# 128-row first projections, lead-in loads on SyncE, and row copies moved or dropped in a memory-augmented attention and gated feed-forward training step

## The chip, the cores and the metric

One core of a Trainium2 chip runs the whole program: forward pass and all gradients in one launch. The metric is the device time of one execution in microseconds (us); below 0.3% a difference can hardly be told from none.

The core has five engines with a program of their own: TensorE (matmuls; PE in the profile, its weight loads PEld), VectorE (DVE), ScalarE (ACT), GpSimd (POOL) and SyncE (SP), which here only starts transfers. Transfers run on 16 DMA engines that all queues share. SyncE, ScalarE and GpSimd each start transfers in the order of their own program: what waits in such a queue holds back what is written behind it.

## The reference

```python
def _fwd_reference(A_x, A_mem0, A_Wq, A_Wk, A_Wv, A_Wo, A_seg_len, B_x, B_w1, B_w3, B_w2):
    xn = _layernorm(A_x)                                   # 2048 x 640
    s = _A_ref(xn, A_mem0, A_Wq, A_Wk, A_Wv, A_Wo, 32)
    g = _silu(_B_ref(xn, B_w1, B_w3, B_w2))                # gated feed-forward, F = 1728
    return A_x + s * g

# _A_ref: 64 segments of 32 tokens, one after another
for s in range(n_seg):
    h = concatenate([mem, xs])                             # 8 memory rows + 32 tokens
    q, k, v = h @ Wq, h @ Wk, h @ Wv                       # 32 heads of 128
    p = softmax(where(mask, q @ k.T * scale, -1e9))
    o = (p @ v) @ Wo
    mem = o[:8]; outs.append(o[8:])
```

The program returns this output and, for a given gradient of it, the gradients of x, mem0, Wq, Wk, Wv, Wo, w1, w3 and w2. All data are bfloat16. The eight memory rows make the 64 segments a chain, forward and again backward.

## The kernel before

The work runs in stages, and within each the order is written out by hand: `in_order` ties every instruction to the one before it on its engine. So the order of the calls in the source is the order of each queue.

**Feed-forward and layer norm** (`phase12_ln_Bfwd`, to about 285 us). Four blocks of 512 tokens; for each of 14 slices of the hidden width, `hidden` multiplies with w1 and w3, and `up` follows one block behind. The normalized rows go to DRAM as XN. Stores of `sl` (to SLT) are on SyncE, of `ds` (to DUT) and of the hidden block (to HB) on GpSimd. In block 3 `x_rows` (L252, L254) copies XN within DRAM into HRO, which has 120 rows per tile: 96 tokens of three segments, then their 24 memory rows. The stage ends with the projections of the first 672 tokens by Wv: `first_rows` (L367 the matmuls, L372 the store) for six blocks of 112 rows and four groups of 1024 columns, in two halves of 512. Here all halves use the PSUM tag `pg`, which has two buffers.

**First part** (`first_part`, 285 to 406 us). The same projections by Wk and then Wq. A counter n runs over the 48 calls of `first_rows`, and other work hangs on its values: fetches of Wq and Wo on ScalarE's queue, `turn_w` (TensorE turns a head of Wv, SyncE stores it to WVT), `kload` and `kturn` of the first keys, the load of vt. The stores go through GpSimd.

**Recurrence forward** (its last Wv matmuls at 1616 us) and **output rows** (to 1795 us), not touched. The recurrence uses `packed_half` (L307): the 32 rows of h against four column groups at once, each in its own 32 columns of the array.

**Recurrence backward** (`phase4_Abwd`, 1795 to 2994 us). A unit is one tile of 120 rows (tl) and four heads (qd). A lead-in works through 19 units: `ld` loads q, v, the gradient and the probabilities, `turn` transposes (its copy gvT has two buffers and is stored to VTD by GpSimd, L1268), `dprob`, `dsoft`, `gmem` follow. The first six units are loaded ahead. In the lead-in, the loads of QVM, QVS or QVX and PR are on GpSimd, that of the gradient and the store GXP (L1315) on SyncE. Then 64 steps of `chain` follow, with later units in their gaps. After each of the first steps from t = 53 downward, one transfer of the list `later` is started on GpSimd (L1406); the first two copy the rows of GS within DRAM into GWO, which is laid out like HRO. Each step stores its gOT stage to GOS on SyncE (L1157) and its eight memory rows to GWO.

**Attention weight gradients** (`phase6_Awgrads`, 2994 to 4224 us). For each of eight groups of four heads, 22 units: loads on SyncE, `s1` to `s4` on TensorE, then `wg` (L1562), which needs the rows hr (loaded from HRO in the first group, L1627). `ld_w` loads the turned weights of a group: Wv from WVT, Wk and Wq by a transposing DMA (L271) from the inputs. GWO is read at the end of the stage.

**Other gradients** (to 4795 us), not touched.

Of the kernel before, what the change touches and what calls it, by code (L numbers as in the profile page):

```python
# [10 lines left out]
F32 = mybir.dt.float32  # L11
# [29 lines left out]
class K:  # L41
# [109 lines left out]
    def setup_dram(self):  # L151
        tc = self.tc
        S, D, T, H, F = self.S, self.D, self.T, self.H, self.F
        HD = self.HD
        dp = self.ctx.enter_context(tc.tile_pool(name="scratch", bufs=1, space=bass.MemoryType.DRAM))
        self.dp = dp
        mk = lambda name, shape, dt=BF16: dp.tile(list(shape), dt, name=name, uniquify=False)
        self.XN = mk("XN", (S, D))
        self.SLT = mk("SLT", (F, S))
        self.DUT = mk("DUT", (F, S))  # L160
        self.HB = mk("HB", (F, S))
        self.DZ = mk("DZ", (S, D))
        self.GB = mk("GB", (S, D))
        self.GS = mk("GS", (S, D))

        self.NR = S + 8 * T
        self.GXA = mk("GXA", (S, D))
        self.HRO = mk("HRO", (self.NR, D))

        self.OT0 = 7  # L170
        self.NO = 4 * ((T - 1 - self.OT0) // 4)
        self.OTX = mk("OTX", (self.NO, P, H, 24))
        self.FS = mk("FS", (T, 64, 320))
        self.SR = mk("SR", (S, D))
        self.GWO = mk("GWO", (self.NR, D))


        self.QVS = mk("QVS", (T // 4, 4, 32, 4, 2, 1024))
        self.KS = mk("KS", (T // 4, 4, 32, 4, 1024))
        self.GOS = mk("GOS", (T // 4, 4, 32, 4, 1024))  # L180
        self.QM = mk("QM", (T, 8, HD))
        self.QVM = mk("QVM", (T, 8, 4, 2, 1024))
        self.NB0 = 672
        self.QVX = mk("QVX", (self.NB0, 2, HD))
        self.KX = mk("KX", (self.NB0, HD))
        self.GB0 = 1344
        self.GL = 2 * P
        self.GX0 = mk("GX0", (S - self.GB0, HD))
        self.OR = mk("OR", (self.NTL * 120, HD))
        self.PR, self.DSR, self.VTD = [], [], []  # L190
        self.GXP = mk("GXP", (self.NTL, P, 8, 3, 2, 32), F32)
        for tl in range(self.NTL):
            n = self.geo(tl)[3]
            self.PR.append(mk(f"PR{tl}", (n, H, P)))
            self.DSR.append(mk(f"DSR{tl}", (n, H, P)))
            ns, nm = self.geo(tl)[0:2]
            self.VTD.append(mk(f"VTD{tl}", (P, ns, H, 40)))
        self.PM = mk("PM", (T, P, 80))
        self.GSP = mk("GSP", (8, 3, 160, 512))
        self.WVT = mk("WVT", (P, H, D))  # L200

    def x_src(self, tl, w, c0, c1):
        return self.tok_src(96 * tl, self.geo(tl)[2], w, c0, c1)
# [43 lines left out]
        r = 120 * (t // 3) + self.geo(t // 3)[2] + 8 * (t % 3)  # L247
        return A[r:r + 8, :]

    def x_rows(self, A, X, eng):  # L250
        n = self.NTL - 1
        eng.dma_start(A[0:120 * n, :].rearrange("(t r) d -> t r d", r=120)[:, 0:96],  # L252
                      X[0:96 * n, :].rearrange("(t r) d -> t r d", r=96))
        eng.dma_start(A[120 * n:120 * n + 32, :], X[96 * n:self.S, :])  # L254


    def g_src(self, tl, c0, c1):
        nx = self.geo(tl)[2]
# [96 lines left out]
    return pt  # L355


def first_rows(k, ps, stage, xs, off, W, dst, x0, cg, nb=112, tag="b0pb", w=1024, q=None):

    nc = k.nc  # L360
    for b in range(2):
        c0 = cg * 1024 + b * 512
        if w == 512 or b == 0:
            st = stage()
        pb = ps.tile([nb, 512], F32, name="b0pb", tag=tag)
        for dc in range(k.DC):
            nc.tensor.matmul(pb[:], xs[:, dc, x0 - off:x0 - off + nb], W[:, dc, c0:c0 + 512],  # L367
                             start=(dc == 0), stop=(dc == k.DC - 1))
        s0 = b * 512 if w == 1024 else 0
        k.copy(st[:, s0:s0 + 512], pb[:], eng='vs'[b])  # L370
        if w == 512 or b == 1:
            (q or nc.sync).dma_start(dst[x0:x0 + nb, cg * 1024 + (b * 512 if w == 512 else 0):cg * 1024 + b * 512 + 512], st[:])  # L372


def phase3_Afwd(k, W4, Wv, Wk_):
# [18 lines left out]
def first_part(k, Wv, Wk_, Wq, Wo, kTs, vt, hxs, rest):  # L394
    nc, tc = k.nc, k.tc
    DC, H, HD = k.DC, k.H, k.HD
    with tc.tile_pool(name="b0", bufs=1) as io, tc.tile_pool(name="b0s", bufs=4) as stp, \
# [50 lines left out]
            turn_w()  # L448
        n = 0
        for W, dst in ((Wk_, k.KX[:, :]), (Wq, k.QVX[:, 0])):  # L450
            for x0 in range(0, k.NB0, 112):
                for cg in range(4):
                    if n % 2 == 1 and fetch:
                        nc.scalar.dma_start(*fetch.pop(0))
                    first_rows(k, ps, lambda: stp.tile([112, 1024], BF16, name="b0st", tag="b0st"), xs, 0, W, dst, x0, cg, q=nc.gpsimd)
                    turn_w()
                    if zero:
                        nc.gpsimd.memset(zero.pop(0)[:], 0.0)
                    if n >= 26 and n % 2 == 0 and (n - 26) // 2 < 9:
                        i = (n - 26) // 2  # L460
                        if i > 0:
                            kturn(i - 1)
                        if i < 8:
                            kload(i)
                    if n == 20:
                        mem_ld()
                    if n == 30:
                        assert not turns
                        nc.gpsimd.memset(kTs[1][:], 0.0)
                    if n == 44:  # L470
                        for i in range(2):
                            nc.sync.dma_start(vt[64 * i + 8:64 * i + 40, :], k.QVX[0:32, 1, 2048 * i:2048 * i + 2048])
                    n += 1
# [432 lines left out]
def phase3b_out(k, Wo, W0, W4):  # L906
# [12 lines left out]
    with tc.tile_pool(name="oio", bufs=1) as io, tc.tile_pool(name="oac", bufs=1, space=bass.MemoryType.PSUM) as pa, \  # L919
# [96 lines left out]
        while g0:  # L1016
# [2 lines left out]
        in_order(k, start)  # L1019
    WT["v"] = W4.tile([P, H, D], BF16, name="WvT", tag="w3")  # L1020

    n = k.NTL - 1
    later = [(k.GWO[0:120 * n, :].rearrange("(t r) d -> t r d", r=120)[:, 0:96], k.GS[0:96 * n, :].rearrange("(t r) d -> t r d", r=96)),
             (k.GWO[120 * n:120 * n + 32, :], k.GS[96 * n:k.S, :])]

    for s in range(3):
        t0 = (2, 0, 1)[s]
# [14 lines left out]
def phase4_Abwd(k, out2, WoT, WvT, WkT, WqT, later):  # L1042
# [3 lines left out]
    with tc.tile_pool(name="gst", bufs=1) as st, tc.tile_pool(name="gchain", bufs=1) as ch, \  # L1046
# [185 lines left out]
        def ld(tl, qd, eng=None):  # L1232

            ns, nm, nx, n = k.geo(tl)
            c0, h0 = qd * 512, qd * 4
            i = cnt["l"]
            cnt["l"] += 1
            early = i < len(pro)
            g = i % 6 if early else (i - len(pro) + 1) % NG
            if g < NG:  # L1240
                gor = gors[g][:]
                qv = fl.tile([120, 2, 512], BF16, name="gqv", tag="gqv", bufs=4)[:]
                Pr = fl.tile([120, 4, P], BF16, name="gPr", tag="gPr", bufs=4)[:]
            else:
                x = xb[:, g - NG]
                qv = x[:, 0:1024].rearrange("p (i c) -> p i c", i=2)
                gor = x[:, 1024:1536]
                Pr = x[:, 1536:2048].rearrange("p (h c) -> p h c", h=4)
            t0 = 3 * tl
            q = nc.gpsimd if early else nc.sync  # L1250
            q.dma_start(
                qv[nx:n], k.QVM[t0:t0 + ns, :, qd // 2, :, 512 * (qd % 2):512 * (qd % 2) + 512].rearrange("t r i c -> (t r) i c"))
            k.load_x(qv, 0, k.x_src(tl, "qv", c0, c0 + 512), q)
            k.load_x(gor, 0, k.g_src(tl, c0, c0 + 512), nc.sync)
            q.dma_start(Pr[0:n], k.PR[tl][:, h0:h0 + 4, :])
            uu["l", tl, qd] = qv, gor, Pr

        def turn(tl, qd):
# [152 lines left out]
def phase6_Awgrads(k, X, out0, out3, out4, out5):  # L1411
# [12 lines left out]
    with tc.tile_pool(name="h6i", bufs=3) as io, tc.tile_pool(name="h6", bufs=1) as hp, \  # L1424
# [20 lines left out]
        def ld_w(qd):  # L1445
            c0 = qd * 512
            ws = []
            for i, src in enumerate((k.A_Wv, k.A_Wk, k.A_Wq)):
                w = gp.tile([P, 4, D], BF16, name="w6", tag=f"w6{i}")
                if i == 0:  # L1450
                    nc.sync.dma_start(w[:], k.WVT[:, 4 * qd:4 * qd + 4, :])
                else:
                    turned_load(k, w[:], src.rearrange("d h e -> d (h e)")[:, c0:c0 + 512])
                ws.append(w)
# [146 lines left out]
        for qd in range(8):  # L1601
            u0 = NTL * qd
            for p in range(NTL):
# [20 lines left out]
                    spill(qd, p - 5)  # L1624
                if 6 <= u < 11:
                    c = 4 * (u - 6)
                    nc.sync.dma_start(hr[0:120, c:c + 4], k.HRO[120 * c:120 * c + 480, :].rearrange("(t p) d -> p t d", p=120))  # L1627
                if u == 11:
                    nc.sync.dma_start(hr[120:P], k.HRO[120 * NF:k.NR, :].rearrange("(t r) d -> r t d", r=8))
                if p % 11 == 2:  # L1630
                    out_ld(2 * qd + p // 11)
                if p % 11 == 6:
# [84 lines left out]
def phase12_ln_Bfwd(k: K, Wv, Wk_):  # L1717
# [6 lines left out]
    with tc.tile_pool(name="bw", bufs=1) as wp, tc.tile_pool(name="bio", bufs=2) as io, \  # L1724
# [128 lines left out]
        for blk in range(NBLK):  # L1853
            for fc in range(FC):
# [20 lines left out]
                if fc == 9:  # L1875
                    fetch((blk + 1) % NBLK)
                if blk == 3 and fc == 2:
                    k.x_rows(k.HRO, k.XN, nc.sync)
                if blk > 0:
                    if fc == 0:  # L1880
                        hidden_out(blk - 1)
# [5 lines left out]
                            up_ld(blk - 1, fc // 2 + 1)  # L1887
        hidden_out(NBLK - 1)
        xb = io.tile([P, DC, BLK], BF16, name="xnT_b", tag="xnT_b")
        turned_load(k, xb[:, :, 0:224], k.XN[448:672, :])  # L1890
        up_ld(NBLK - 1, 0)
        up_ld(NBLK - 1, 1)
        xa, off = xnTs[NBLK], 0
        stg = []

        def stage():
            stg.append(ln.tile([112, 512], BF16, name="b0st", tag=f"xt{len(stg) % 8}"))
            return stg[-1]
        for n, (x0, cg) in enumerate([(x0, cg) for x0 in range(0, k.NB0, 112) for cg in range(4)]):
            if n % 3 == 1 and n // 3 < TB:  # L1900
                up(NBLK - 1, n // 3)
                if n < 6:
                    up_ld(NBLK - 1, n // 3 + 2)
            if x0 == 448:
                xa, off = xb, 448
            first_rows(k, ps, stage, xa, off, Wv, k.QVX[:, 1], x0, cg, tag="pg", w=512)
        in_order(k, start)


# [271 lines left out]
```

## Time and profile before

Median of three runs 4798.12 us (4796.45 to 4808.65); the profiled execution took 4796.79 us, its span is 4795.1 us.

| stretch, us | what | TensorE busy, us | granted clock | DMA share |
|---|---|---|---|---|
| 180 to 190 | feed-forward, block 3 | 3.28 of 10 | 0.75 | 0.44 |
| 250 to 300 | Wv projections, change of stage | 43.30 of 50 | 1.00 | 0.41 |
| 300 to 350 | first part, Wk | 48.27 of 50 | 1.00 | 1.02 |
| 350 to 400 | first part, Wq | 50.00 of 50 | 1.00 | 0.47 |
| 1800 to 1810 | backward lead-in, start | 4.51 of 10 | 0.50 | 0.53 |
| 1840 to 1850 | backward lead-in | 5.54 of 10 | 0.83 | 1.10 |
| 2078 to 2110 | backward steps, GWO copy | 23.86 of 32 | 0.79 | 0.72, then 0.55 |
| 3000 to 3020 | weight gradients, start | 7.57 of 20 | 0.50 | 1.13, then 0.99 |
| 3110 to 3150 | wg of the first group | 39.84 of 40 | 1.00 | 0.24 |

The granted clock is the share of TensorE's full speed that it was given; the DMA share is the mean busy share of the 16 DMA engines (it can come out a little over 1). A line of the timeline gives start, duration, engine, source line, operation, output and input tiles, the number of instructions, and in brackets the idle time before it with what ended it. A line of the waits reads: who waited, for whom, us in total, times, longest. A line of a table by stretches gives TensorE, weight loads, VectorE, ScalarE and GpSimd busy us with counts, the clock, the DMA share and GB/s.

### The profile page before, as it was taken

How to read it: one execution, taken by the hardware profiler on the slowest of the kernel's cores; microseconds unless marked ns; L12 is line 12 of the kernel's file. 1: busy time of each engine (PE TensorE's matmuls, PEld its weight loads, DVE VectorE, ACT ScalarE, POOL GpSimd, SP SyncE). 2: the span in 40 equal slices, each digit the busy share in tenths (PEclk: the TensorE clock that was granted, in tenths of full speed). 3: DMA queues.
4: the chain of work that ended last, by engine and by line, in shares of the span. 5: the costliest groups of instructions: out<-in, count | busy, mean ns of one | idle time of the engine just before them, and what ended most of it. 6: DMA issues, size and time to landing. Idle time of an engine off the chain costs nothing. (4 is left out here: it accounts for less than half of the span.)

```text
span 4795.1 us, 160346 instructions
## 1 busy us (share of the span) xinstructions
PE 4474.0 (93%) x64434; PEld 2864.5 (60%) x64704; DVE 2248.3 (47%) x7164; ACT 1591.1 (33%) x4371; POOL 2109.1 (44%) x3541
## 2 busy tenths in 40 slices
PE   8898999999999787989999998899999999999999
PEld 4455555555555464656666665666666666667665
DVE  8634666666666524545555553332234322311460
ACT  5432555555544522323333332322233222300000
POOL 6522555555555405445544443643355433411340
PEclk9999999999999796999999999899999999999999
DMA  8763566666555497777777773943455433669774
GB/s 271 234 231 101 174 178 180 179 181 181 178 166 169 128 218 206 209 210 207 219 210 208 212 211 111 207 131 108 108 151 154 133 109 106 190 193 223 158 179 98
DMA packets 997844, 841.31 MB, mean 175 GB/s; under 512 B 542558, under 2 KB 880402, under 8 KB 995096
## 3 DMA queue, kind: packets, MB, share of 16 engines
q1 hardware_dynamic: 784201, 552.53, 41.9%
q0 software_dynamic: 130592, 229.98, 16.4%
q10 hardware_dynamic: 82307, 48.52, 3.9%
q8 instruction: 511, 8.37, 0.8%
q14 instruction: 233, 1.91, 0.1%
HBM read 473.80 MB, written 311.48 MB: 164 GB/s over the span
## 5 line engine op out<-in xcount | busy, mean ns | idle before, releaser
L1562 PE MATMUL wg<-gr,hr 128*128 128x512 bf16 x2352 | 519.1, 379 | 2.5
L1543 PE MATMUL g<-w,ghacc 128*128 128x320 bf16 x3072 | 459.8, 300 | 0.8
L1562 PEld LDWEIGHTS <-hr 128*128 128x128 bf16 x2400 | 233.9, 98 | 278.8
L1543 PEld LDWEIGHTS <-ghacc 128*128 128x128 bf16 x3072 | 288.4, 98 | 104.2 <-ACT ghacc L92 2.2
L307 PEld LDWEIGHTS <-hx 128*32 128x32 bf16 x7680 | 176.7, 96 | 168.9 <-issue 5.7
L90 DVE CAST wgo<-wg 128x512 bf16<-128x512 f32 x72 | 49.8, 692 | 471.3 <-PE wg L1562 462.9
L90 DVE CAST stg<-bank 128x512 bf16<-128x512 f32 x256 | 177.0, 692 | 161.4 <-PE bank L307 154.9
L778 POOL DMA_DIRECT2D OR<-xv x163 | 90.4, 555 | 354.0 <-ACT xv L92 334.0
L92 ACT COPY ghacc<-t6g 128x768 bf16<-128x768 bf16 (+1 forms) x176 | 137.2, 780 | 304.1 <-PE t6g L1525 303.1
L1508 POOL DMA_DIRECT2D GSP<-grs x48 | 25.7, 547 | 477.6 <-ACT grs L1500 474.8
L326 PEld LDWEIGHTS <-gkv 128*8 128x8 bf16 x8192 | 179.0, 87 | 89.0 <-issue 7.1
L1268 POOL DMA_DIRECT2D VTD<-gvT x176 | 129.4, 741 | 219.7 <-ACT gvT L1267 199.9
L730 POOL TENSOR_TENSOR xP<-xP,xrz 120x480 bf16<-120x480 bf16 x163 | 161.4, 990 | 75.1 <-DVE xrz L729 46.2
L710 ACT ACTIVATE xP<-xsp,xnm 120x120 bf16<-120x120 f32 (+1 forms) x540 | 186.6, 373 | 20.5 <-DVE xnm L692 17.2
L1549 DVE TENSOR_TENSOR ghacc<-ghacc,g 128x320 f32<-128x320 f32 x192 | 93.5, 487 | 210.0 <-PE g L1543 210.0
L92 ACT CAST wgo<-wg 128x512 bf16<-128x512 f32 x48 | 28.1, 586 | 479.8 <-PE wg L1562 421.4
L1297 DVE SCALAR_TENSOR_TENSOR gdS<-gdp,Dx,gPr 120x120 bf16<-120x120 f32 (+1 forms) x680 | 182.8, 331 | 0.0
L326 PE MATMUL bank<-Wo,oTm 128*32 128x320 bf16 x4032 | 158.2, 312 | 18.8 <-DVE oTm L608 18.8
L326 PE MATMUL gbank<-WvT,gkv 128*8 128x320 bf16 x4096 | 171.0, 311 | 4.6 <-issue 3.6
L1315 POOL DMA_DIRECT2D GXP<-gks x157 | 91.1, 581 | 190.9 <-ACT gks L1313 184.3
L326 PE MATMUL gbank<-WkT,gkv 128*8 128x320 bf16 x4096 | 163.9, 301 | 3.9 <-issue 2.1
L307 PE MATMUL bank<-Wq,hx 128*32 128x512 bf16 x2560 | 163.0, 384 | 2.6 <-DVE stg L90 2.6
(354 smaller groups left out, 10920.6 us busy)
## 6 DMA issues: line engine op xcount, KB each, us to landing
QVS<-stg SPq DMA_DIRECT2D x128, 256.0 KB
vTt<-VTD SPq DMA_DIRECT2D x64, 320.0 KB
VTD<-gvT POOLq DMA_DIRECT2D x168, 120.0 KB, 3.8
DSR<-gdS POOLq DMA_DIRECT2D x168, 120.0 KB, 3.2
dS<-DSR SPq DMA_DIRECT2D x168, 120.0 KB
P<-PR SPq DMA_DIRECT2D x168, 120.0 KB
PR<-xP POOLq DMA_DIRECT2D x163, 120.0 KB, 3.3
OR<-xv POOLq DMA_DIRECT2D x163, 120.0 KB, 3.1
```

Of the source, the lines that this page charges most:

```text
L90: return nc.vector.tensor_copy(out, in_)
L92: return nc.scalar.copy(out, in_)
L307: k.nc.tensor.matmul(bank[32 * g:32 * g + 32, :], x[:, dc, :], W[:, dc, c0:c0 + 512], start=(dc == 0), stop=(dc == k.DC - 1), tile_positio ...
L326: k.nc.tensor.matmul(pm[p0:p0 + nq, 0:320], x[:, h, :], W[:, h, 320 * b:320 * b + 320], start=(first and i == 0), stop=(last and i == 15), ...
L710: nc.scalar.activation(Pb[0:n, j, 0:n], sp[0:n, j, :], ACT.Exp, bias=nmx[0:n, j:j + 1], scale=k.scale, accum_out=Z[0:n, j:j + 1])
L730: eng.tensor_tensor(Pb[0:n, :, 0:n], Pb[0:n, :, 0:n], bc_last(rz[0:n], n), ALU.mult)
L1268: nc.gpsimd.dma_start(k.VTD[tl][:, :, h0:h0 + 4, :], vTq[:])
L1297: nc.vector.scalar_tensor_tensor(dS[0:n, j, 0:n], dp[0:n, j, :], Dx[0:n, j:j + 1], Pr[0:n, j, 0:n], op0=ALU.subtract, op1=ALU.mult)
L1315: (nc.sync if (tl, qd) in pro else nc.gpsimd).dma_start(k.GXP[tl, :, qd, 0:ns], ks[:].rearrange("p s i h m -> p s i (h m)"))
L1543: nc.tensor.matmul(pg[:], ring[:, i, j, r0:r0 + P], Ws[qd][i][:, j, 320 * h:320 * h + 320], start=(i == 0 and j == 0), stop=(i == 2 and j ...
L1549: nc.vector.tensor_tensor(a, a, pg[:], ALU.add)
L1562: nc.tensor.matmul(pw[:], hr[:, tl, dc * P:(dc + 1) * P], grs[i][:, tl, :], start=(tl == 0), stop=(tl == NF - 1))
```

## The change

Five edits. The first 672 tokens are cut into five blocks of 128 rows and a rest of 32 rows, which `last_rows` does packed, four column groups at once; in the feed-forward stage the two halves get a PSUM tag each. The values of n move with the smaller number of calls (42), and the last stores (n from 36) go through SyncE. The lead-in loads of QVS or QVX and of PR go through SyncE. The copy of XN into HRO is dropped but for the last two tiles; hr takes its 96 token rows from XN. The copy of GS into GWO is cut into eight pieces, one behind unit 18 of each head group (the seventh group has two, the last none), and in its old place the first head group of the turned Wk and Wq is stored to a new DRAM tensor WQK, from which `ld_w(0)` loads it. What the edits are for: fewer rows of the array left unused, a shorter GpSimd queue, and no large DRAM copies or transposing loads at points where the order of the work leaves little slack.

```diff
-def first_rows(k, ps, stage, xs, off, W, dst, x0, cg, nb=112, tag="b0pb", w=1024, q=None):
+def first_rows(k, ps, stage, xs, off, W, dst, x0, cg, tag="b0pb", w=1024, q=None):
...
-        pb = ps.tile([nb, 512], F32, name="b0pb", tag=tag)
+        pb = ps.tile([P, 512], F32, name="b0pb", tag=tag if isinstance(tag, str) else tag[b])
...
+def last_rows(k, ps, stage, xs, off, W, dst, tag="b0pb", w=1024, q=None):
+    x0 = k.NB0 - 32
+    for b in range(2):
+        if w == 512 or b == 0:
+            st = stage()
+        pb = ps.tile([P, 512], F32, name="b0pb", tag=tag if isinstance(tag, str) else tag[b])
+        packed_half(k, pb, xs[:, :, x0 - off:x0 - off + 32], W, b)
+        s0 = b * 512 if w == 1024 else 0
+        k.copy(st[:, s0:s0 + 512], pb[:], eng='vs'[b])
+        if w == 512 or b == 1:
+            c0, c1 = (b * 512 if w == 512 else 0), b * 512 + 512
+            (q or k.nc.sync).dma_start(dst[x0:k.NB0].rearrange("r (g c) -> g r c", g=4)[:, :, c0:c1], st[:])
...
-            for x0 in range(0, k.NB0, 112):
-                for cg in range(4):
+            for x0 in list(range(0, k.NB0 - 32, P)) + [None]:
+                for cg in range(4 if x0 is not None else 1):
...
+                    if x0 is None:
+                        last_rows(k, ps, stage, xs, 0, W, dst, q=nc.gpsimd if n < 36 else nc.sync)
+                    else:
+                        first_rows(k, ps, stage, xs, 0, W, dst, x0, cg, q=nc.gpsimd if n < 36 else nc.sync)
...
-    later = [(k.GWO[0:120 * n, :].rearrange("(t r) d -> t r d", r=120)[:, 0:96], k.GS[0:96 * n, :].rearrange("(t r) d -> t r d", r=96)),
-             (k.GWO[120 * n:120 * n + 32, :], k.GS[96 * n:k.S, :])]
+    later = [(k.WQK[i], WT[w][:, 0:4, :]) for i, w in enumerate("kq")]
...
-            k.load_x(qv, 0, k.x_src(tl, "qv", c0, c0 + 512), q)
+            k.load_x(qv, 0, k.x_src(tl, "qv", c0, c0 + 512), nc.sync)
             k.load_x(gor, 0, k.g_src(tl, c0, c0 + 512), nc.sync)
-            q.dma_start(Pr[0:n], k.PR[tl][:, h0:h0 + 4, :])
+            nc.sync.dma_start(Pr[0:n], k.PR[tl][:, h0:h0 + 4, :])
...
-                if i == 0:
-                    nc.sync.dma_start(w[:], k.WVT[:, 4 * qd:4 * qd + 4, :])
+                if i == 0 or qd == 0:
+                    nc.sync.dma_start(w[:], k.WVT[:, 4 * qd:4 * qd + 4, :] if i == 0 else k.WQK[i - 1])
...
-                    nc.sync.dma_start(hr[0:120, c:c + 4], k.HRO[120 * c:120 * c + 480, :].rearrange("(t p) d -> p t d", p=120))
+                    nc.sync.dma_start(hr[0:96, c:c + 4], k.XN[96 * c:96 * c + 384, :].rearrange("(t p) d -> p t d", p=96))
+                    nc.sync.dma_start(hr[96:120, c:c + 4], k.HRO[120 * c:120 * c + 480, :].rearrange("(t p) d -> p t d", p=120)[96:120])
...
+                if p == 18:
+                    if qd < 7:
+                        nc.gpsimd.dma_start(k.GWO[360 * qd:360 * qd + 360, :].rearrange("(t r) d -> t r d", r=120)[:, 0:96],
+                                            k.GS[288 * qd:288 * qd + 288, :].rearrange("(t r) d -> t r d", r=96))
+                    if qd == 6:
+                        nc.gpsimd.dma_start(k.GWO[120 * NTL - 120:120 * NTL - 88, :], k.GS[96 * NTL - 96:S, :])
...
-                    k.x_rows(k.HRO, k.XN, nc.sync)
+                    k.x_rest(k.HRO, k.XN, nc.sync)
...
-            first_rows(k, ps, stage, xa, off, Wv, k.QVX[:, 1], x0, cg, tag="pg", w=512)
+            first_rows(k, ps, stage, xa, off, Wv, k.QVX[:, 1], x0, cg, tag=("pg", "pu"), w=512)
+        last_rows(k, ps, stage, xb, BLK, Wv, k.QVX[:, 1], tag=("pg", "pu"), w=512)
```

## The prediction

> **What bounds the kernel now.** The page first: the busy table and the chain that ended last.
>
> ```profile
> PE 4474.0 (93%) x64434; PEld 2864.5 (60%) x64704; DVE 2248.3 (47%) x7164; ACT 1591.1 (33%) x4371; POOL 2109.1 (44%) x3541
> ```
>
> TensorE has work on record 93% of the span, so time can go in two ways only: fewer matmul microseconds, or fewer holes between them. I went through TensorE's timeline stage by stage where the diff touches it, then asked the waits and the queues of SyncE and GpSimd what ended each hole.
>
> The first projections run TensorE flat out, at a granted clock of 1.00:
>
> ```profile
> 376.77 4.49 PE L367 MATMUL b0pb<-Wq,b0x 128*112 128x512 bf16 x20
> 381.10 0.34 PE L443 MATMUL kpt<-ident,kr 96*128 96x96 bf16 x4
> 381.27 4.49 PE L367 MATMUL b0pb<-Wq,b0x 128*112 128x512 bf16 x20
> ...
> 414.53 1.25 PE L307 MATMUL bank<-Wv,hx 128*32 128x512 bf16 x20
> ```
>
> From 376.77 to 381.10 twenty matmuls take 4.33 us, 0.216 each, whether 112 rows are used or 128. The last line, from the recurrence, is the packed form: twenty matmuls of 32 rows, four side by side, follow one another every 1.19 us (414.53, 415.71 the next).
>
> The same projections with Wv, at the end of the feed-forward stage, have holes:
>
> ```profile
> 242.71 1.24 PE L367 MATMUL b0pb<-Wv,xnT_b 128*112 128x512 bf16 x5 [0.72 <-ACT b0st L92]
> 244.28 3.40 PE L367 MATMUL b0pb<-Wv,xnT_b 128*112 128x512 bf16 x15 [0.33 <-DVE b0st L90]
> ```
>
> Both halves share one PSUM tag of two buffers, and ScalarE is late while it serves `up`.
>
> The two copies from DRAM to DRAM leave the widest holes:
>
> ```profile
> 188.69 2.29 PE L1784 MATMUL pg<-xnT_b,w1s 128*128 128x512 bf16 x5 [6.67 <-DVE sl L1793]
> ```
> ```profile
> 2078.00:2094.00 16.00, 12.38 (x266) 7.68 (x263) 6.70 (x36) 3.94 (x13) 6.72 (x13) 0.79 0.72 245
> 2094.00:2110.00 16.00, 11.48 (x197) 7.00 (x199) 2.64 (x8) 4.14 (x13) 4.97 (x9) 0.79 0.55 168
> 2110.00:2126.00 16.00, 15.30 (x371) 10.16 (x365) 9.31 (x50) 5.46 (x19) 8.14 (x16) 1.00 0.78 228
> ```
> ```profile
> POOL GXP L1315 <- DMA GWO<-GS: 5.7, 1, 5.7
> ```
>
> The first hole follows the HRO copy (issued at 162.8, 2520 KB read and written again): VectorE waits for buffers whose stores stand in the full rings. The second begins where GWO<-GS is issued (2078.62): TensorE falls from 15.3 busy us of 16 to 12.4 and 11.5, and the clock from 1.00 to 0.79.
>
> The lead-in of the backward recurrence, and the start of the weight gradients:
>
> ```profile
> 1810.32 0.55 POOL L1255 DMA_DIRECT2D krb<-PR  x1
> 1810.86 0.58 POOL L1268 DMA_DIRECT2D VTD<-gvT  x1
> ```
> ```profile
> ACT gvT L1266 <- DMA VTD<-gvT: 39.4, 11, 9.1
> ```
> ```profile
> 3001.92 5.56 SPq L271 DMA_TRANSPOSE w<-in_A_Wk_dram  x1
> 3007.53 5.91 SPq L271 DMA_TRANSPOSE w<-in_A_Wq_dram  x1
> 3013.48 0.60 SPq L1462 DMA_DIRECT2D dS<-DSR  x1
> ```
> ```profile
> 3016.57 0.58 PE L1483 MATMUL t<-ident,dS 120*128 120x120 bf16 x4 [11.48 <-DMA dS<-DSR]
> ```
>
> GpSimd issues eighteen loads before its first VTD store, for which ScalarE then waits. Later, two weight transposes hold SyncE for 11.5 us, and the load for which TensorE idles 11.48 us stands behind them.
>
> **What the skill says.** "TensorE: Matmul & The Clock Gate", Part 3: four column tiles run at once, its three-tile case measured 2.38 times; this trace gives 4.33/1.19 = 3.6 times for four. Same page, Part 1: after an idle window of some 3.4 us the clock falls to half; agreed, the five matmuls behind the 6.67 us hole took 2.29 us against 1.24. "DMA: Bandwidth & Descriptors", section Issuing engines are not separate DMA queues: another issuing engine saves only sequencer time; so I give the move to SyncE nothing in bandwidth. No SyncE landing is listed in this trace, so for a load I use that page's fit (Anatomy of one DMA): 2.0 us + bytes/436 GB/s.
>
> **The change, part by part.**
>
> *1. Rows.* Per weight, 6 blocks x 8 halves x 5 = 240 matmuls become 5 x 8 x 5 = 200 plus two packed halves of 20. Before: 48 x 1.08 = 51.8 us. After: 40 x 1.08 + 2 x 1.19 = 45.6. Saved 6.2 per weight; all on the path, since TensorE is the engine that ends these stretches: 18.7 for three weights. Evictions fall from 48 to 42 halves per weight at 0.69 (VectorE) or 0.59 us (ScalarE) and stay hidden: a pair of halves takes 2.16.
>
> *2. Two PSUM tags for Wv.* The waits for b0st between 216 and 256 (0.70, 0.34, then 0.72 and about 0.33 three times) add up to 4.2 us; four banks cover them. Saved 4.
>
> *3. Give-back in the first part.* From 300 to 345 the DMA share is 1.01 to 1.06, at 370 to 414 GB/s, with TensorE full since 315. The same bytes must now move in about 7 us less, and Wq is needed 7 us earlier. Its last piece is issued at 315.4, its first use was 351.8; slack remains. The last stores go through SyncE, where two kr loads now stand behind stores that wait for evictions; the turn two chunks later (4.3 us) needs them. Cost 0 to 6; I take 2.
>
> *4. No HRO copy of the rows.* Gone: 6.67 and 1.47 us of holes, and 3.7 - 2.2 = 1.5 from the half clock afterwards: 9.7. Blocks 1 and 2 keep 1 to 1.8 at the same place without such a copy. Saved 8 (6 to 10). The later hr loads read the same bytes in ten loads instead of five: five more issues of 0.43 us on SyncE, spread over five units.
>
> *5. GWO copy moved.* The distances of the GOS stores, one per step, are 17.8, 31.5 and 13.0 around the copy, 62.3 for three steps; neighbours take about 17.0. Excess 11.2. The two WQK stores in its place move 640 KB each, an eighth of the copy's 5040 KB both ways: at most 2 x 11.2/8 = 2.8; in 5 KB rows I take 1. Saved 10 (8 to 11). In the weight-gradient stage eight pieces of about 360 KB each come just ahead of the wg matmuls, where the DMA share is 0.24 (3110 to 3150) and loads run five units ahead. If each cost in proportion, 11.2/7 = 1.6, it would be 12; I take 1.
>
> *6. Lead-in loads.* GpSimd loses two of five issues per unit (1.1 us). Six QVM issues end at about 1804, so VTD can go when its tile is ready, some 5 us before 1810.86; the 4.09 us hole at 1816 should go. SyncE gets twelve more issues at the front (12 x 0.45 = 5.4 us), before WvT, which only the recurrence needs. Behind that, ScalarE's VTD waits could lose 11 x 1.1 = 12, but the DMA share here is 0.72 to 1.10, and TensorE is at half clock. Saved 5, ends -5 and 17. On SyncE each added wait for a free buffer now holds back the GX loads and GXP stores behind it; they have six units of lead.
>
> *7. WQK instead of two transposes.* SyncE frees 11.5 - 0.9 us. Each 640 KB load is an estimate of 2.0 + 1.5 = 3.5 us, but three units (1.8 MB) and WVT share the rings, so the dS load lands at about 3010 instead of 3016: 6 to 7. Thereafter the DMA share is 0.94 to 1.07 until 3080, which may give some back. Saved 6 (2 to 11).
>
> Sum: 18.7 + 4 - 2 + 8 + 10 - 1 + 5 + 6 = 48.7. Prediction 4798 - 49 = 4749.
>
> **The rivals.**
>
> *A, the DMA takes it back.* Where the share is at 1, TensorE only waits elsewhere: parts 6 and 7 give 0 and 2, part 3 costs 6, part 5's pieces 6, part 4 gives 6. Sum 18.7 + 4 - 6 + 6 + 10 - 6 + 0 + 2 = 29, time 4769. For it: the saturated stretches. Against: 1, 2 and 5 lie where the DMA isn't full.
>
> *B, more than counted.* The lead-in runs warm and the VTD waits go: part 6 gives 17, part 7 11, part 5 11. Sum 18.7 + 4 - 2 + 10 + 11 - 0 + 17 + 11 = 70, time 4728. For it: clocks of 0.50 to 0.66 in the lead-in. Against: 23 MB have to move there in 100 us, with engines busy some 80%.
>
> *C, slower.* SyncE becomes the lead-in's bound: three more issues in each of 21 steps, 3 x 21 x 0.45 = 28 lost, the eight pieces cost 12, Wq comes 10 late, and the copies' holes stay for other stores (parts 4 and 5 give 0). With part 7 at 2: 18.7 + 4 + 2 - 28 - 12 - 10 = -25, time 4823. Against: SyncE would issue about 2.2 us in a step of 3.9.
>
> **How the numbers follow.** Forecast 0.58, A 0.21, B 0.15, C 0.06. The range reaches from B to a little beyond A, 4728 to 4775. Faster by over 0.3% means under 4783.7: the forecast, B and nearly all of A, 0.90; within 0.3% 0.05; slower 0.05.
>
> **What would show it.** 1: 40 halves of 1.08 us per weight and two of 1.2; the stretch from the first Wv projection (208.9) to the first recurrence matmul (405.7), 196.8 us now, shorter by 20 or more. 2: no b0st wait of TensorE near `up`. 4: no hole over 2 us in block 3. 5: all step distances near 17, and no hole at the eight pieces. 6: the first VTD store about 5 us after its first load. 7: dS right behind WQK in SyncE's queue, and the 11.48 us hole about halved. The prediction is wrong if holes of the same size appear in the first part or the lead-in, ended by KX, Wq or QVS transfers, or if the moved pieces delay units.

## The result and the profile after

The changed kernel takes 4753.68 us (median of four, 4748.53 to 4760.77), the kernel before on the same chip 4797.28: ratio 0.991, 95% interval 0.9883 to 0.9937. Forecast were 4749 us, and a saving of 48.7; the medians differ by 43.6, the spans of the two profiled executions by 44.2 (4795.1 and 4750.9).

TensorE stays the bound. Its row of the page after:

```profile
PE 4482.5 (94%) x64704; PEld 2829.5 (60%) x64704; DVE 2241.5 (47%) x7155; ACT 1586.0 (33%) x4362; POOL 2085.1 (44%) x3499
```

Busy TensorE time didn't fall (4474.0 before). The records of before lack 270 matmuls and an interval of back-to-back matmuls includes modelled tails, so this row can't tell rows saved from holes closed. I therefore cut both spans at the same TensorE events, rounded their positions to 0.1 us and compared the distances:

| from, to | before, us | after, us | gain | forecast |
|---|---|---|---|---|
| start, first Wv projection | 208.9 | 200.0 | 8.9 | 8 (part 4) |
| to the first turn of Wv | 74.9 | 62.7 | 12.2 | 10.2 (part 2, a third of part 1) |
| to the first Wk projection | 5.5 | 8.6 | -3.1 | 0 |
| to the first recurrence matmul (h by Wk) | 116.4 | 105.7 | 10.7 | 10.4 (rest of part 1, part 3) |
| to h by Wq | 4.9 | 7.8 | -2.9 | 0 |
| to the recurrence's last Wv matmul | 1205.7 | 1206.7 | -1.0 | 0 |
| to the lead-in's first transpose | 187.9 | 191.5 | -3.6 | 0 |
| to the first step of `chain` | 79.7 | 74.4 | 5.3 | 5 (part 6) |
| to its last | 1093.7 | 1081.7 | 12.0 | 10 (part 5) |
| to the first unit of the weight gradients | 19.8 | 20.1 | -0.3 | 0 |
| to its first wg | 109.6 | 107.4 | 2.2 | 6 (part 7) |
| eight head groups | 1117.1 | 1115.7 | 1.4 | -1 (part 5's pieces) |
| to the end | 571.0 | 568.6 | 2.4 | 0 |

Stretches that no edit touches scatter too: the recurrence took 1200.7 to 1211.4 us over the twelve profiles of this study with changed code. The stretch from the first Wk projection to the recurrence took 105.0 to 109.6 us over the same twelve, so its gain of 10.7 is near the upper end of 6.8 to 11.4. So a difference of 2 us in a long stretch says nothing; in the short ones a hole has to be named.

TensorE's timeline at the Wv projections, after:

```profile
199.97 2.32 PE L366 MATMUL b0pb<-Wv,xnT_b 128*128 128x512 bf16 x10
...
205.93 6.92 PE L366 MATMUL b0pb<-Wv,xnT_b 128*128 128x512 bf16 x30
...
237.62 22.03 PE L366 MATMUL b0pb<-Wv,xnT_b 128*128 128x512 bf16 x100
259.58 2.34 PE L306 MATMUL b0pb<-Wv,xnT_b 128*32 128x512 bf16 x40
...
271.25 4.42 PE L366 MATMUL b0pb<-Wk,b0x 128*128 128x512 bf16 x10 [5.32 <-DMA b0x<-XN]
```

The b0st holes near the `up` calls have gone (one of 0.73 us, 0.72 before, is left at the first turn of Wv), one hundred matmuls follow one another, and the 32-row rest takes 2.34 us for forty. The last line has a hole of 5.32 us where before had 2.20:

```profile
289.26 2.34 PE L367 MATMUL b0pb<-Wk,b0x 128*112 128x512 bf16 x10 [2.20 <-DMA b0x<-XN]
```

The longer hole costs more than its length: behind it the granted clock is 0.50 from 271 to 274 us, and the first two groups of ten matmuls take 4.42 and 2.72 us, where before they took 2.34 and 2.32. Another new hole of the first part, 1.97 us at 343.14, ends with the first load of kr from KX. In block 3 (160 to 200 us) TensorE has no hole at all; the 6.67 us one has gone.

The table by stretches in which the WQK stores stand in the GWO copy's place (issued at 2051.73 and 2069.72), columns as before:

```profile
2052.00:2068.00 16.00, 13.69 (x338) 9.13 (x341) 7.31 (x38) 4.57 (x18) 6.24 (x12) 1.00 0.88 230
2068.00:2084.00 16.00, 15.32 (x368) 9.78 (x360) 7.80 (x38) 5.52 (x17) 8.22 (x15) 1.00 0.77 237
2084.00:2100.00 16.00, 15.85 (x387) 10.79 (x388) 9.18 (x49) 5.84 (x21) 8.64 (x16) 1.00 0.70 208
```

The clock stays at 1.00; the three steps that were 17.8, 31.5 and 13.0 us apart are now 17.5, 18.3 and 17.2. That is 9.3 of the 12.0 us; the rest is spread over the other steps.

GpSimd's queue in the lead-in, and the waits of ScalarE there:

```profile
1784.14 0.60 POOL L1284 DMA_DIRECT2D VTD<-gvT  x1
```
```profile
ACT gks L1329 <- DMA GXP<-gks: 23.1, 8, 4.5
...
POOL gox L1103 <- DMA gride<-GS: 12.4, 1, 12.4
...
ACT gvT L1282 <- DMA VTD<-gvT: 8.0, 3, 6.0
```

The first VTD store is issued 1.1 us after the lead-in's first transpose (1783.00); before it was 6.6 us after (1804.23, 1810.86). The wait for VTD fell from 39.4 to 8.0 us. But a wait for GXP, which before's list of waits in this stretch does not hold, has taken its place (20.1 of its 23.1 us lie inside the lead-in), and GpSimd's wait for gride grew from 5.7 to 12.4. Both transfers are on SyncE's queue.

SyncE's queue and TensorE's hole at the start of the weight gradients:

```profile
2963.70 0.95 SPq L1467 DMA_DIRECT2D w<-WQK  x2
2964.69 0.70 SPq L1478 DMA_DIRECT2D dS<-DSR  x1
```
```profile
2975.59 0.58 PE L1499 MATMUL t<-ident,dS 120*128 120x120 bf16 x4 [9.18 <-DMA dS<-DSR]
```

SyncE is free 10.6 us sooner, and yet the hole shrank only from 11.48 to 9.18: the dS load now takes 10.9 us from its issue to its use, where it took 3.1. While TensorE idles, from 2966 to 2975 us, the DMA share is 1.01 to 1.06.

### The profile page after: what moved, and what is told of

Same layout as the page of the kernel before. It is cut to its first block, busy times and chain, and to the rows that moved or that the text cites. A ratio compares the mean times of both kernels' runs of the same rounds, so it can differ in the third digit from the quotient of the medians.

```text
span 4750.9 us, 160544 instructions
## 1 busy us (share of the span) xinstructions
PE 4482.5 (94%) x64704; PEld 2829.5 (60%) x64704; DVE 2241.5 (47%) x7155; ACT 1586.0 (33%) x4362; POOL 2085.1 (44%) x3499
## 5 line engine op out<-in xcount | busy, mean ns | idle before, releaser
L748 POOL TENSOR_TENSOR xP<-xP,xrz 120x480 bf16<-120x480 bf16 x163 | 161.2, 989 | 75.6 <-DVE xrz L747 47.1
L728 ACT ACTIVATE xP<-xsp,xnm 120x120 bf16<-120x120 f32 (+1 forms) x540 | 186.6, 374 | 20.8 <-DVE xnm L710 17.5
```

The lines of the kernel that those rows point to most:

```text
L728: nc.scalar.activation(Pb[0:n, j, 0:n], sp[0:n, j, :], ACT.Exp, bias=nmx[0:n, j:j + 1], scale=k.scale, accum_out=Z[0:n, j:j + 1])
L748: eng.tensor_tensor(Pb[0:n, :, 0:n], Pb[0:n, :, 0:n], bc_last(rz[0:n], n), ALU.mult)
```

## The experiments

All start from the changed kernel. Times are set against the kernel before on the same chip. For the parts I use the distances of the table, since parts of 2 to 6 us are below what a few executions of 4750 us resolve. Each kernel has one profile.

### 1 and 2. The last store: its form or its queue

TensorE's hole at the start of the recurrence, before and after, and what holds it, on VectorE's timeline after:

```profile
410.58 2.33 PE L307 MATMUL bank<-Wq,hx 128*32 128x512 bf16 x20 [2.58 <-DVE stg L90]
```
```profile
384.77 2.32 PE L306 MATMUL bank<-Wq,hx 128*32 128x512 bf16 x20 [5.43 <-DVE stg L90]
```
```profile
384.03 1.29 DVE L90 CAST stg<-bank 128x512 bf16<-128x512 f32 x2 [7.12 <-DMA QVX<-b0st]
```

VectorE's first copy of the recurrence waits for the landing of the last first-part store, issued on SyncE at 377.89: 6.1 us later. In the kernel before, the same copy (at 409.84) had waited 4.40 us for a QVX store: the wait is an old one, the change made it longer. That store has a form of its own, four groups of 32 rows in one transfer. The first kernel splits it; the second only moves it to another queue.

```diff
-            (q or k.nc.sync).dma_start(dst[x0:k.NB0].rearrange("r (g c) -> g r c", g=4)[:, :, c0:c1], st[:])
+            for g in range(4):
+                (q or k.nc.sync).dma_start(dst[x0:k.NB0, 1024 * g + c0:1024 * g + c1], st[32 * g:32 * g + 32, :])
```

> The changed kernel, but last_rows stores its 128 partitions as four transfers of 32 rows each, one per column group, in place of one transfer whose outermost dimension has four entries. Theory (the single store runs on a few DMA engines only and lands late): the hole in front of the second projection of the recurrence falls from 5.43 us to 3 or less, the wait for the turned rows b0x ahead of the Wk projections from 5.32 us to about 2 to 3; about 5 to 6 us off the changed kernel, 4748. Rival (the late landing comes from SyncE's queue, or from issuing later): both holes stay as they are, within 1 us, time unchanged.

```diff
-                        last_rows(..., q=nc.gpsimd if n < 36 else nc.sync)
+                        last_rows(..., q=nc.gpsimd)
```

> The changed kernel, with the 32-row store of Wq issued by GpSimd instead of SyncE, in the same form with four outer entries. Theory (its form makes it slow): the 5.43 us hole at the start of the recurrence stays, between 4.5 and 6.5. Rival (the move of the store to SyncE made it slow): the hole goes back to the 2.58 us of the kernel before. Time within 3 us of the changed kernel either way.

Measured: 4763.49 us (4751.77 to 4767.14; ratio 0.9917, 0.9887 to 0.9947) and 4753.68 (0.9909, 0.9874 to 0.9944). VectorE and TensorE in the first:

```profile
381.15 1.29 DVE L90 CAST stg<-bank 128x512 bf16<-128x512 f32 x2 [4.32 <-DMA QVX<-b0st]
```
```profile
381.90 1.26 PE L306 MATMUL bank<-Wq,hx 128*32 128x512 bf16 x20 [2.62 <-DVE stg L90]
```

TensorE in the second:

```profile
388.63 2.33 PE L306 MATMUL bank<-Wq,hx 128*32 128x512 bf16 x20 [6.83 <-DVE stg L90]
```

Split, the same 256 KB are released 3.3 us after the first issue (377.82), and TensorE's hole falls from 5.43 to 2.62 us, before's 2.58. On GpSimd, still as one transfer of four groups, it is 6.83. So it is the form, not the queue. A reason is in the Trainium skill, "DMA: Bandwidth & Descriptors", section Rules for kernel authors: the engines of a transfer are set by its slowest dimension, so one whose outermost dimension has four entries runs on at most four. The trace fits this: the DMA share is 0.15 from 380 to 385 us in the changed kernel, under the 0.25 that four of sixteen would make, and 0.33 in the split one; which engines ran, no view lists.

The other hole, 5.32 us at the first Wk projection, did not fall: it is 5.80 in the split kernel. There the rest is two stores, so eight issues in its place took SyncE 3.58 us from 261.82 instead of 1.55, and the b0x loads came out of SyncE no sooner (266.96 against 267.02). So for this hole the form is not shown to be the cause. Nor did the time follow: 4748 was expected of the split kernel, and it came out 10 us above the second on the same chip, whose hole at the recurrence is longer.

### 3. The rows alone

Everything but the 128-row projections, their two PSUM tags and the queue of the last stores is put back as before.

> The kernel before with the rows part alone: 128-row blocks, packed rest, two PSUM tags for Wv, last stores on SyncE; both DRAM copies, the lead-in loads on GpSimd and the transposed weight loads as before. Theory (parts add up, as the ledger of the two traces has it): Wv stretch shorter by 11 to 12 us, first part by 10 to 11, minus 3 and 4 at the two changes of stage: 15 to 16 us off the kernel before, 4782. Rival (the DMA takes it back once the copies are there too): 8 us or less, 4790.

Measured: 4789.58 us over 20 executions (before 4799.5 over 28; 0.9978, 0.9967 to 0.9989). By the h by Wq matmul the profile is 16.6 us ahead of before (394.0 against 410.6): 1.5 by the first Wv projection, 12.2 at Wv, 9.4 in the first part, less 3.6 at the change of weights and 2.9 at the start of the recurrence. At the end it is 10.3 ahead: its recurrence took 1210.6 us and its backward steps 1097.9, both long among the profiles. Code that no edit touches took those 6 us. I can't tell whether by chance. So the parts are those of the theory (15 to 16 us), but the time, 9.9 us off, is the one that the rival named, 4790, and the rings are not shown to be its reason.

### 4. The GWO copy put back

```diff
+    later += [(k.GWO[0:120 * n, :]..., k.GS[0:96 * n, :]...),
+              (k.GWO[120 * n:120 * n + 32, :], k.GS[96 * n:k.S, :])]
...
-                if p == 18:
-                    if qd < 7:
-                        nc.gpsimd.dma_start(k.GWO[360 * qd:360 * qd + 360, :]..., k.GS[288 * qd:288 * qd + 288, :]...)
...
```

> The changed kernel, with the copy of GS into GWO back in the list of the backward recurrence (behind the two WQK stores) and no pieces in the weight gradient stage. Theory: three neighbouring step distances add up to about 11 us more than three usual ones, and the head groups of the weight gradients keep their distance of about 149 to 150 us; 10 to 12 us above the changed kernel, 4764. Rival (the eight pieces cost there what the copy had cost): groups get shorter by 1 to 1.6 us each, and the time stays within 3 us of the changed kernel.

Measured: 4783.8 us (9 executions; 0.9959, 0.9945 to 0.9973). The steps of `chain` take 1095.3 us instead of 1081.7, and the step around the copy is 30.5 us long again. The stretches by time, for the copy's issue at 2092.34 and what follows:

```profile
2092.00:2108.00 16.00, 12.71 (x263) 8.18 (x260) 6.66 (x35) 3.33 (x11) 3.83 (x7) 0.79 0.67 247
2108.00:2124.00 16.00, 9.38 (x160) 6.79 (x161) 3.65 (x18) 4.16 (x16) 7.22 (x15) 0.79 0.60 174
```

TensorE loses its work and its clock for two stretches, as before. The head groups take 1117.0 us without the eight pieces and 1115.7 with them: no cost of theirs shows. In the changed kernel, with the piece issued at 3060.26 in flight, the DMA share is 0.66 over 10 us, and TensorE stays busy for all of them. The same bytes cost 13.6 us in one piece in the backward steps and none in eight in the weight gradients. The time is further off than these steps: 10 to 12 us above the changed kernel were expected, the spans of the profiles differ by 24.3. The 10.7 us beyond the steps lie scattered over the other stretches (3.2 of them at the start of the weight gradients), and no run says why. The transfers in the two places also meet different neighbours; cutting and moving weren't tried apart.

### 5. The HRO copy put back

The loop of `x_rest` becomes the two copies of `x_rows` again, and hr comes from HRO in five loads.

> The changed kernel with the whole copy of XN into HRO back in block 3, and hr loaded from HRO in five loads. Theory: the hole of some 6.7 us in block 3 and the half clock behind it come back, and the Wv projections start 8 to 9 us later than in the changed kernel; nothing moves at the hr loads (within 2 us over the first head group). Rival (the hole came from elsewhere, for example the HB store): the Wv projections start within 2 us of the changed kernel.

Measured: 4768.32 us (0.9931, 0.9906 to 0.9956). TensorE in block 3:

```profile
192.30 2.29 PE L1807 MATMUL pg<-xnT_b,w1s 128*128 128x512 bf16 x5 [6.62 <-DVE sl L1816]
...
205.75 1.24 PE L1807 MATMUL pg<-xnT_b,w1s 128*128 128x512 bf16 x5 [1.34 <-DVE sl L1816]
```

Both holes are back, of before's size; the first Wv projection starts at 212.5 instead of 200.0. Some 2 us of this lay behind already at 53 us (55.0), and 2.8 at the start of block 3 (156.8 against 154.0), ahead of the copy, so the copy costs about 10. What passes the delay on is in the waits of this kernel:

```profile
POOL DUT L1823 <- DMA HB<-hBT: 12.3, 1, 12.3
DVE ds L1819 <- DMA DUT<-ds: 9.8, 1, 9.8
```

With the copy in flight, the stores that GpSimd starts from 166.8 to 176.1 us land only between 190.0 and 193.2. The first of them, of the hidden block (HB), takes 23.1 us (23.0 in the kernel before, 7.9 in the changed one). VectorE waits for the source buffer of one of these stores (ds), and TensorE waits for VectorE; GpSimd, too, issues its next DUT store only when HB has landed. The stretch with the hr loads is the same with five loads as with ten (107.5 and 107.4).

### 6. The lead-in's loads back on GpSimd

```diff
-            k.load_x(qv, 0, k.x_src(tl, "qv", c0, c0 + 512), nc.sync)
+            k.load_x(qv, 0, k.x_src(tl, "qv", c0, c0 + 512), q)
...
-            nc.sync.dma_start(Pr[0:n], k.PR[tl][:, h0:h0 + 4, :])
+            q.dma_start(Pr[0:n], k.PR[tl][:, h0:h0 + 4, :])
```

> The changed kernel with the lead-in loads of QVS or QVX and of PR back on GpSimd. Theory: the lead-in, from its first transpose to the first chain matmul, goes from 74.4 us back to about 79.7, the first VTD store stands behind eighteen loads again and the hole of about 4 us after the fourth unit returns. Rival (the DMA sets the pace and the two traces differ by chance): 73 to 76 us, as now.

Measured: 4756.51 us (three executions; 0.9908, 0.9863 to 0.9953). GpSimd's queue, TensorE's timeline and ScalarE's waits:

```profile
1788.28 0.58 POOL L1284 DMA_DIRECT2D VTD<-gvT  x1
```
```profile
1793.84 0.19 PE L1297 MATMUL gdp<-gvT,gOT 128*128 128x8 bf16 x1 [3.32 <-ACT gOT L1289]
```
```profile
ACT gvT L1282 <- DMA VTD<-gvT: 38.0, 11, 8.4
...
POOL gox L1103 <- DMA gride<-GS: 3.9, 1, 3.9
...
ACT gks L1329 <- DMA GXP<-gks: 2.3, 1, 2.3
```

The hole behind the first VTD store and the 38 us of VTD waits return; the GXP wait falls from 23.1 to 2.3 and the gride wait from 12.4 to 3.9. So the move itself exchanged one wait of ScalarE for another. The lead-in takes 77.7 us against 73.3 to 75.6 in the ten kernels that have these loads on SyncE: the exchange leaves 2 to 4 us. The 79.7 expected was not reached; the two other kernels with these loads on GpSimd, before and the third, take 79.7 and 80.2, and what makes their last 2 us is not shown.

### 7 and 8. Why the weight gradients start no sooner

The seventh kernel loads Wk and Wq by the transposing DMA again; its WQK stores stay and aren't read. The eighth puts the three weight loads behind two more units.

```diff
-                if i == 0 or qd == 0:
+                if i == 0:
```

> The changed kernel with the first head group's Wk and Wq loaded by transposing transfers again; the WQK stores stay but are not read. Theory (bytes on the rings, not SyncE's time, set the start): from the first transpose of the weight gradients to the first wg matmul 109 to 110 us against 107.4, about 2 more. Rival (SyncE's 11.5 us set it, as the prediction had it): 113 us or more.

```diff
-        ld_to(3)
-        ld_w(0)
         ld_to(5)
+        ld_w(0)
```

> The changed kernel with the three weight loads of the first head group issued behind units 3 and 4 instead of ahead of them. Theory (unit 3 waits for the 2 MB of weights in front of it on the rings): the hole of 9.18 us falls to 4 or less, and the first wg matmul comes 3 to 5 us earlier relative to the first transpose, 102 to 104 us. Rival (the rings are full until the end of the first group and take it back): the hole shrinks, but the distance stays at 106 to 109 us.

Measured: 4760.61 us (0.9907, 0.9868 to 0.9946) and 4766.52 (0.9919, 0.9892 to 0.9946). SyncE's queue and TensorE's hole in the seventh:

```profile
2972.44 5.38 SPq L270 DMA_TRANSPOSE w<-in_A_Wk_dram  x1
2977.87 4.05 SPq L270 DMA_TRANSPOSE w<-in_A_Wq_dram  x1
2981.96 0.59 SPq L1478 DMA_DIRECT2D dS<-DSR  x1
```
```profile
2985.11 0.58 PE L1499 MATMUL t<-ident,dS 120*128 120x120 bf16 x4 [9.46 <-DMA dS<-DSR]
```

With SyncE held for 9.4 us again, the hole is 9.46 us: 0.3 more than the 9.18 without. From the load of WVT to the use of dS are 13.1 us with the transposes (2971.98 to 2985.11) and 12.4 without (2963.23 to 2975.59). In the seventh the dS load is used 3.15 us after its issue, so there SyncE is late; freed of the transposes, the load comes hardly sooner, since the bytes in front of it take as long. The difference is also within the scatter of this hole: 9.5 to 11.5 us in the three profiles with transposes, 8.7 to 10.2 in eight with plain loads (all but kernels 8 and 10). The distance to the first wg is 109.7 us, as before (109.6) and as the theory had it; the ten kernels with plain loads take 104.4 to 110.6, 107.7 on average, so the plain loads are worth some 2 us. TensorE's timeline in the eighth:

```profile
2986.99 0.58 PE L1499 MATMUL t<-ident,dS 120*128 120x120 bf16 x4 [1.22 <-DMA dS<-DSR]
2991.74 1.23 PE L1559 MATMUL g<-w,ghacc 128*128 128x320 bf16 x4 [4.17 <-DMA w<-WVT]
2994.17 1.22 PE L1559 MATMUL g<-w,ghacc 128*128 128x320 bf16 x4 [1.21 <-DMA w<-WQK]
2996.70 1.23 PE L1559 MATMUL g<-w,ghacc 128*128 128x320 bf16 x4 [1.30 <-DMA w<-WQK]
```

The dS hole is down to 1.22 us, and 4.17, 1.21 and 1.30 us of holes for w take its place. The distance to the first wg is 107.4 us, the same as in the changed kernel, as the rival had it. Whichever load comes first, all of them have to pass: in the changed kernel the DMA share is 0.88 from 2960 to 2980, 0.91 and 1.07 in the next two stretches of 20 us. The order moves the hole about and hardly shortens the stretch. (This kernel's backward steps took 1092.1 us, by a few steps of 19 to 22 us in code that the edit doesn't touch; its time is not evidence on the order.)

### 9, 10 and 11. One tag, the rest first, and the changed kernel again

These three ran on one chip, before at 4809.25 us. The ninth takes `tag="pg"` for both halves of Wv again.

> The changed kernel with both halves of the Wv projections on the one PSUM tag of two buffers, as before the change. Theory: the b0st holes near the four up calls return, and the Wv stretch, 62.7 us from its first projection to the first turn of Wv, becomes about 67 to 68. Rival (with 128 rows the evictions keep up): under 64.

Measured: 4767.61 us (two executions; 0.9912, 0.9878 to 0.9947). TensorE at the Wv projections:

```profile
203.81 1.24 PE L366 MATMUL b0pb<-Wv,xnT_b 128*128 128x512 bf16 x4 [1.37 <-DVE sl L1816]
...
211.72 1.24 PE L366 MATMUL b0pb<-Wv,xnT_b 128*128 128x512 bf16 x5 [0.71 <-ACT b0st L92]
213.30 3.40 PE L366 MATMUL b0pb<-Wv,xnT_b 128*128 128x512 bf16 x14 [0.34 <-DVE b0st L90]
```

The stretch takes 68.5 us instead of 62.7, a little more than expected. Of these 5.8, 4.2 are the b0st holes (0.71 to 0.72 four times, about 0.33 four times), and 1.37 is a hole ended by sl, the last user of the tag `pg` ahead of the projections.

The tenth does the 32-row rest ahead of the last block, for all three weights, so that its store is no longer the last one.

```diff
-            for x0 in list(range(0, k.NB0 - 32, P)) + [None]:
+            for x0 in [0, 128, 256, 384, None, 512]:
...
+            if n == 16:
+                last_rows(k, ps, stage, xb, BLK, Wv, k.QVX[:, 1], tag=("pg", "pu"), w=512)
...
-        last_rows(k, ps, stage, xb, BLK, Wv, k.QVX[:, 1], tag=("pg", "pu"), w=512)
```

> The changed kernel with the packed 32-row rest computed ahead of the last 128-row block instead of behind it, for all three weights, so that the last store of each stretch is an ordinary one of 128 rows. Theory (the rest's store, on few DMA engines, is late where the next stage waits for it): the hole at the second projection of the recurrence falls from 5.43 to about 2.6 us, the distance from the first turn of Wv to the first Wk projection from 8.6 to about 6; 5 to 6 us below the changed kernel on the same chip. Rival (the change of stage costs the same, since other stores or loads are in flight then): distances stay within 1 us, time the same.

> The changed kernel once more, beside the one with the rest first, on the same chip. Theory: 0.990 to 0.992 of the kernel before, first part near 105 to 108 us, as in its other profiles.

Measured: 4751.53 us for the rest first (4748.67 to 4760.13; 0.9884, 0.9862 to 0.9906), 4760.12 for the changed kernel again (4752.93 to 4769.25; 0.9897, 0.9875 to 0.992). TensorE with the rest first:

```profile
270.69 3.68 PE L366 MATMUL b0pb<-Wk,b0x 128*128 128x512 bf16 x9 [3.40 <-DMA b0x<-XN]
...
381.83 1.26 PE L306 MATMUL bank<-Wq,hx 128*32 128x512 bf16 x20 [1.52 <-DVE stg L90]
```

In the changed kernel on the same chip the hole at the first Wk projection is 5.70 us and that at the start of the recurrence 5.46; here they are 3.40 and 1.52, and h by Wq comes at 381.8 us instead of 386.7. That is 4.9 us gained by the order of two calls, close to the 5 to 6 expected, and this is the version with the lowest ratio of all. In its new place the store costs nothing: the Wv stretch takes 62.8 us (62.7), the first part 107.3 (107.2). The intervals of the two ratios overlap, so the times alone don't prove it; the holes do.

## Why the prediction came out right

The time (4749 forecast, 4753.68 measured) is right in the main for the reasons given, with one term clearly too large and one cost missed. That it is so close is in part luck: in the table, the rows that gained more than forecast make up 10.3 us, those that gained less 14.7. By the prediction's own parts:

1. *Rows.* Right. The first part gained 10.7 us (forecast 12.4 less 2; 6.8 to 11.4 over the twelve profiles), and at Wv 12.2 - 5.8 = 6.4 (forecast 6.2). Of the sign named for it, 20 or more off the 196.8 us from the first Wv projection to the recurrence, 19.8 came, just short: the missed cost below took it.
2. *Two tags.* Right in mechanism, 4 forecast, 5.8 measured by undoing it. The sum took in the holes that end with b0st only. The 1.36 us hole at 211.51 us, ended by sl, belonged to the same tag and was left out.
3. *Give-back.* The 2 us fit the first part's 10.7 by luck: what was lost there is some 2.7 us of half clock behind the 5.32 us hole and the 1.97 us hole at the first kr load. Against this, three small holes of before (1.62, 1.07 and 0.59 us) have shrunk to two (0.30 and 0.66). The late stores were looked at for the two kr loads behind them, which left no hole in this profile. What stood there was VectorE's first copy of the recurrence, and it waits for the last store to land. The missed term: a new form of store as the last one of a stretch, -3.1 us at the change of weights, with the half clock behind it, and -2.9 at the start of the recurrence. Kernel 10 shows for both that it comes of being last; kernels 1 and 2 show for the second that it is the form. The form was in the diff, and the 4.40 us wait of before was in the trace.
4. *No HRO copy.* Right: 8 forecast, 8.9 measured, about 10 by undoing it (kernel 5), inside the range given. VectorE did wait for stores that were long issued. But the rings were not full for all that time: before, in the hole, the DMA share is 0.22 from 180 to 184 us and 0.45 from 184 to 188. What held these stores so long is not shown.
5. *GWO copy moved.* Right in mechanism: 10 forecast (8 to 11), 12.0 measured, 9.3 of them at the copy's own three steps, and 13.6 by undoing it. For the pieces 1 was taken off; no cost of theirs shows (kernel 4). Rival A's 6 for them is rejected.
6. *Lead-in.* Right size (5 forecast, 5.3 measured; 2 to 4 by undoing it). The first VTD store came 5.5 us sooner relative to the first transpose. The upper end, 17, assumed that ScalarE's VTD waits go and nothing comes instead. They went, from 39.4 to 8.0, and 23.1 us of GXP waits came: the stated "six units of lead" hold for the loads, not for the GXP store, whose source buffer ScalarE needs again. This is the new wait that rival C feared, without its 28 us.
7. *WQK.* The mis-sized term: 6 forecast, 2.2 measured, at the lower end of 2 to 11 and within the scatter of that stretch. The failed step is "the dS load lands at about 3010 instead of 3016: 6 to 7". It let SyncE's 10.6 us count, and took the landing from the skill page's fit, which is for one DMA started by GpSimd: 3.5 us for 640 KB, where 120 KB behind 1.9 MB of other loads took 10.9 from issue to use. Kernels 7 and 8, and the DMA share of 1.01 to 1.06 in the hole, show that the loads of this stage together set the time, in whatever order and almost as much with as without the transposes. Of the two signs named, dS came right behind WQK, but the hole was not halved.

Of the rivals, A was right about part 7 alone, and B about part 5. What stays open is the 3.6 us by which the untouched output rows took longer: all profiles with changed code have this stretch 1.4 to 5.7 us over the one profile of before, the kernel with the rows alone too. No run singles out a cause.

## What to carry to other kernels

When an edit gives a transfer a new shape, ask first who waits for it to land: here the same bytes were free in the middle of a stage and cost 2 to 4 us as its last store. Shortening a queue helps only as far as the queue ends the wait; where the DMA share is near 1 behind it, sum the bytes of the stage instead of the issues. A large copy from DRAM to DRAM is worth avoiding, or cutting and putting where the rings have room: here one dropped and one cut and moved gave 9 to 14 us each, at no cost that the traces show. Look for what such a copy delays in the waits of all the queues: here it was the stores of another queue, and through them two engines.

## What the runs showed of the hardware

- 256 KB stored as one transfer of four groups of 32 rows were released 6.1 us after issue, with the DMA share at 0.15 from 380 to 385 us; as four transfers of 32 rows, 3.3 us after the first issue.
- A plain 640 KB load costs SyncE 0.48 us in the changed kernel (two in 0.95), a transposing one 4.05 to 5.91 us (kernel 7 and before). In a stage bound by its bytes TensorE's hole was 9.5 to 11.5 us with two transposing loads and 8.7 to 10.2 with plain ones.
- Four column groups of 32 rows run at 40 matmuls in 2.17 us (374.84 to 377.01, start to start) and 2.27 (252.22 to 254.49, with the rest first), 0.054 to 0.057 us each against 0.216 for one of 128 rows: a factor of 3.8 to 4.0, more than the 3.6 that I read from before.
- With a 2520 KB copy from DRAM to DRAM issued beside it, the store HB<-hBT took 21 to 23 us to land (before, kernels 3 and 5), and 7.9 in the changed kernel without the copy.
